# Three small moves in an attention and feed-forward kernel: VectorE's order of sums, a fifth block's PSUM bank, and the split of one product

## The chip, the cores and the metric

One core of a Trainium2 chip. The metric is the device time of one execution in microseconds, lower is better; medians of several runs are quoted. Times are compared within the same rounds.

A ratio of two kernels is the mean time of the one's runs over the mean of the other's in the same rounds, so it is not quite the ratio of the medians.

## The reference, cut to what matters

```python
# q, k, v: (8, 8, 1024, 64); E, F: (64, 1024); w_in: (512, 2048); w_out: (2048, 512)
k_proj = E @ k;  v_proj = F @ v                      # per batch and head, 1024 -> 64
attn   = softmax(q @ k_proj.T / 8)                   # 64 columns
x      = (attn @ v_proj), heads side by side         # (8192, 512)
h      = np.maximum(x @ w_in, 0.0)
out    = (h * h) @ w_out                             # float32
```

## The kernel before: the parts that the change touches

The kernel goes through 8 batches `b`; each has two chunks `ch` of 512 tokens. A chunk has a first stage (16 blocks of `x @ w_in`, each 4 matmuls of 512 columns, then ReLU on ScalarE and the square on VectorE) and a second stage, which makes `(h*h) @ w_out` with seven products in place of eight: the quarters of `h*h` are first added and subtracted on VectorE (the "sums" `s0` to `s3`), as are those of `w_out` (`T1` to `T4`). Attention of the next batch is put between the steps of both stages. The tiles `ps_...` lie in PSUM banks: the kernel's matmuls write them, and ScalarE or VectorE then reads them (VectorE's add of a `ps_y` tile at 79.00 us of the profiled run takes 0.68 us).

```python
def sums(hsq, s, q4, which):          # q4: first or second half of the feature blocks
    ...
    for o, x, y, op in (
        (0, a21, a22, ALU.add), (1, s[0][:, js], a11, ALU.subtract),
        (2, a11, a21, ALU.subtract), (3, a12, s[1][:, js], ALU.subtract),
    ):
        if o in which:
            nc.vector.tensor_tensor(out=s[o][:, js], in0=x, in1=y, op=op)
...
def operands_after(k):                # after the square of pair k
    if b and 4 <= k < 7:
        operands(0, (k - 4,))
    if b and k == 7:
        operands(0, (3,))
        operands(1, (0,))
...
def step1(k, n):
    ...
    if b < 2 or k % 2:
        ps = ffn_psum("ps_h")         # 4 banks in batches 0 and 1, one block each
    ...
    first(ch, HFB * h + j, ps, range(NCB))
    square(k, n, ps)
...
before = range(2) if (b, ch) == (0, 0) or 1 < b < B - 1 else lo     # lo = range(0, 4)
...
def p2a():                            # first part of the second product
    if b:
        operands(1, (1,))
    product(st["x"], st["A12"], W21, before, True)
def p1c():
    product(st["y"], st["A11"], W11, range(7, 8))
    if b == 1:
        operands(1, (3, 2))
    st["a"] = part_pool.tile([P, 2, MH], F32, name="p_a")
    copy(st["a"], "y")                # ScalarE
def p5(js): ... product(st["z"], st["s"][0], T1[:], js, ...)        # then copy to p_d
def p6(js): ... product(st["y"], st["s"][1], T2[:], js)             # goes on in the bank that p_a was read from
def p7(js): ... product(st["y"], st["s"][2], T3[:], js)             # then VectorE: o1 = y + p_d
def p2b():                            # last part of the second product
    product(st["x"], st["A12"], W21, range(before.stop, HFB))
    add(st["o0"][:, :, 0:MH], "x", st["a"])
    if b > 1:
        operands(1, (2, 3))
    ...
def p4(js): ... product(st["y"], st["A22"], T4[:], js)              # goes on in the bank that VectorE just read
...
# batches 0 and 1:
second = [p1a, p2a, p1b, p1c] + lohi(p5) + lohi(p6) + lohi(p3) + lohi(p7) + [p2b] + lohi(p4)
```

The first, fourth, sixth and seventh products all accumulate in one bank `ps_y` without clearing it, so the kernel has each after the first wait until the copy or add that reads the state before it is through (the add at 79.00 us is through at 79.68, and the next `ps_y` matmul starts at 79.73). In batches 0 and 1, `p2b` (bank `ps_x`) covers the read between `p7` and `p4`, with 0.87 us of matmuls there.

Batch 1's attention is placed by step (32 is the first step of the second stage of chunk (0,0)):

```python
BATCH_1 = {
    33: "project 1", 34: "copy_kp, transpose_q, copy_vp", 37: "copy_v_down",
    48: "scores 0, scores 1, exponentials 0", 49: "exponentials 1",
    51: "scores 2, scores 3, exponentials 2", 52: "exponentials 3",
    ...
```

`project` needs K and V of batch 1, which are loaded behind all weights (in the profiled run the last of the weights is issued at 27.59 us, K at 29.09 and V at 30.38). Its K and V matmuls write different halves of one tile's rows; where both operands are there, the two of a pair start within 5 ns of each other (48 pairs after 56 us in the profiled run). `copy_vp` is two copies on ScalarE.

The softmax here doesn't subtract the row's maximum and nothing guards it: scores larger than these inputs give would overflow.

## Time and profile before

| | before |
|---|---|
| time, median of 3 runs | 482.01 us (481.49 to 482.94) |
| span of the profiled run | 480.1 us |
| TensorE / VectorE / ScalarE busy | 98% / 65% / 52% |
| TensorE without idle time | from 53.30 us to the tail |

The page's busy line, the table of stretches, TensorE's timeline at 20 and 52 us, the chain of waits and VectorE's timeline are shown in the prediction. In the timeline a piece begins where its first instruction starts. In the chain of waits a TensorE piece begins where the piece before it *ends*, some 0.16 us later, since the records of matmuls overlap (one of 512 columns is 379 ns long, the next starts after 216). Lengths agree in both.

### The profile page before, as it was taken

Reading aid. Unit: us, or ns where it says so; the run is one execution under the profiler, and the core shown is the slowest. Engines: PE = TensorE matmul, PEld = TensorE weight load, DVE = VectorE, ACT = ScalarE, POOL = GpSimd, SP = SyncE. Lnnn points to the kernel's source line nnn. Section 1 sums busy time; section 2 is a strip of 40 time slices with the busy share of each in tenths; the row PEclk is TensorE's granted clock in tenths of the full one; section 3 lists DMA queues with packets and bytes.
Section 4 is the critical chain, followed back from the end, with each engine's and each line's share of the span. In section 5 each row is a group of like instructions: output and inputs, shape, how many; then the busy total and the mean of one; then the engine's idle time right before and its main releaser. Section 6 shows DMA issues by size and latency. Waiting matters only on the chain.

```text
span 480.1 us, 8400 instructions
## 1 busy us (share of the span) xinstructions
PE 468.3 (98%) x3630; PEld 294.0 (61%) x3630; DVE 314.4 (65%) x382; ACT 247.8 (52%) x365; POOL 34.8 (7%) x48
## 2 busy tenths in 40 slices
PE   4899999999999999999999999999999999999997
PEld 2544686475664756648475574846657475766656
DVE  1478955554957659584695838857485856959383
ACT  2387544758416564375634756156652666334352
POOL 6440020020020100001000100000000000000000
PEclk9999999999999999999999999999999999999999
DMA  9999989579979997209952199223402002020202
GB/s 159 203 204 207 168 183 200 138 117 226 168 113 239 141 209 140 88 1 147 223 81 89 19 178 206 49 87 62 127 1 82 6 1 88 1 89 0 89 1 87
DMA packets 72789, 55.46 MB, mean 116 GB/s; under 512 B 33968, under 2 KB 64944, under 8 KB 72752
## 3 DMA queue, kind: packets, MB, share of 16 engines
q0 software_dynamic: 30624, 29.36, 39.8%
q1 hardware_dynamic: 42128, 25.56, 21.2%
q8 instruction: 28, 0.46, 0.4%
q14 instruction: 9, 0.07, 0.0%
HBM read 59.24 MB, written 16.78 MB: 158 GB/s over the span
## 4 chain that ended last, share of the span: by engine, by line
PE 88%; DMA 9%; POOL 1%; issue 0%; ACT 0%; POOLq 0%
PE ps_h L507 23%; PE ps_y L527 22%; PE ps_att L507 17%; PE ps_z L527 16%; DMA V_sb<-in_v_dram 7%; PE ps_kv L216 2%; PE ps_att L258 2%; PE ps_att L527 2%; DMA w_in<-in_moe_w_in_dram 2%; PE ps_att L243 2%; PE ps_x L527 1%; PE ps_kv L217 0%; POOL V_sb L120 0%; POOL K_sb L120 0%; POOL Q_sb L124 0%
## 5 line engine op out<-in xcount | busy, mean ns | idle before, releaser
L571 DVE TENSOR_TENSOR hsq<-h_relu 128x1024 bf16<-128x1024 f32 x123 | 149.9, 1222 | 79.1 <-ACT h_relu L563 62.5
L507 PEld LDWEIGHTS <-w_in 128*128 128x128 bf16 x1024 | 99.6, 98 | 117.9 <-issue 1.9
L507 PE MATMUL ps_h<-xT,w_in 128*128 128x512 bf16 x640 | 147.8, 379 | 0.2 <-DVE xT L390 0.2
L527 PEld LDWEIGHTS <-s 128*128 128x128 bf16 x1024 | 99.1, 98 | 16.2 <-issue 4.8
L561 ACT ACTIVATE h_relu<-ps_h 128x512 f32<-128x512 f32 x159 | 92.3, 596 | 24.2 <-PE ps_h L507 24.0
L507 PE MATMUL ps_att<-xT,w_in 128*128 128x512 bf16 x384 | 90.7, 379 | 0.0
L527 PEld LDWEIGHTS <-hsq 128*128 128x128 bf16 x768 | 73.8, 98 | 16.5 <-issue 6.0
L563 ACT ACTIVATE h_relu<-ps_att 128x1024 f32<-128x1024 f32 x48 | 49.1, 1023 | 55.4 <-PE ps_att L507 55.4
L527 PE MATMUL ps_y<-T,s 128*128 128x256 bf16 x480 | 57.7, 273 | 0.0
L521 DVE TENSOR_TENSOR s<-hsq 128x1024 bf16<-128x1024 bf16 x64 | 43.5, 683 | 0.0
L285 DVE TENSOR_TENSOR xT<-ps_att,rs 128x1024 bf16<-128x1024 f32 x28 | 33.0, 1214 | 0.6 <-PE ps_att L258 0.6
L657 DVE TENSOR_TENSOR o_sb<-ps_z,p_b 128x512 f32<-128x512 f32 x16 | 11.1, 691 | 33.4 <-PE ps_z L527 27.5
L527 PE MATMUL ps_z<-T,s 128*128 128x256 bf16 x256 | 30.9, 273 | 0.0
L527 PE MATMUL ps_z<-w_out,s 128*128 128x256 bf16 x256 | 30.7, 273 | 0.0
L527 PE MATMUL ps_y<-w_out,hsq 128*128 128x256 bf16 x240 | 30.5, 273 | 0.0
L651 ACT COPY o_sb<-ps_y 128x512 f32<-128x512 f32 x15 | 8.7, 578 | 40.2 <-PE ps_y L527 40.1
L527 PE MATMUL ps_y<-T,hsq 128*128 128x256 bf16 x240 | 29.0, 273 | 0.0
L250 ACT ACTIVATE expT<-ps_att 128x1024 bf16<-128x1024 f32 x28 | 27.7, 1029 | 1.9 <-PE ps_att L243 1.9
L657 DVE TENSOR_TENSOR o_sb<-ps_y,p_d 128x512 f32<-128x512 f32 x15 | 10.4, 690 | 21.4 <-issue 19.7
L651 ACT COPY p_b<-ps_y 128x512 f32<-128x512 f32 x15 | 8.8, 588 | 27.0 <-PE ps_y L527 27.0
L521 DVE TENSOR_TENSOR s<-s,hsq 128x1024 bf16<-128x1024 bf16 x32 | 21.8, 685 | 0.4
L521 DVE TENSOR_TENSOR s<-hsq,s 128x1024 bf16<-128x1024 bf16 x32 | 21.8, 683 | 0.0
(86 smaller groups left out, 277.4 us busy)
## 6 DMA issues: line engine op xcount, KB each, us to landing
out_dram<-o_sb SPq DMA_DIRECT2D x30, 512.0 KB, 3.4
K_sb<-in_k_dram POOLq DMA_DIRECT2D x7, 1024.0 KB, 10.7
V_sb<-in_v_dram POOLq DMA_DIRECT2D x7, 1024.0 KB, 17.8
Q_sb<-in_q_dram POOLq DMA_DIRECT2D x7, 1024.0 KB, 10.4
w_out<-in_moe_w_out_dram POOLq DMA_DIRECT2D x4, 512.0 KB, 13.8
w_in<-in_moe_w_in_dram POOLq DMA_DIRECT2D x7, 256.0 KB, 10.4
K_sb<-in_k_dram POOLq DMA_DIRECT2D x2, 512.0 KB, 8.3
out_dram<-o_sb SPq DMA_DIRECT2D x3, 256.0 KB, 2.1
```

The costliest lines, as they stand in the source:

```text
L216: nc.tensor.matmul(ps[0:KP, :], lhsT=ET[:, i, :], rhs=kv[:, :, i, :], start=f, stop=l)
L243: nc.tensor.matmul(ps[o, bank, :], lhsT=self.kT[r, 2 * pr + j, :], start=True, stop=True, rhs=self.qT[r, NT * (2 * pr + j):NT * (2 * pr + ...
L250: nc.scalar.activation(e[:], self.ps["s", pr][:], AF.Exp, scale=SCALE)
L285: nc.vector.tensor_tensor(out=self.xT[:, 2 * g + e].rearrange("p a n t -> p a (n t)"), in0=self.ps["v", g, e][:], in1=self.rs[g][:], op=AL ...
L507: nc.tensor.matmul(ps[:], lhsT=w_in_blk(cb, fb), rhs=xT[:, cb, :, 2 * ch:2 * ch + 2], start=(cb == 0), stop=(cb == NCB - 1),)
L521: nc.vector.tensor_tensor(out=s[o][:, js], in0=x, in1=y, op=op)
L527: nc.tensor.matmul(ps[tb] if len(ps) == 2 else ps[0][:, tb], lhsT=lhs[:, j, tb * P:(tb + 1) * P], rhs=rhs[:, j], start=first and n == 0 an ...
L561: nc.scalar.activation(r[:, n], ps[:], AF.Relu)
L563: nc.scalar.activation(r[:], st["h"][:], AF.Relu)
L571: multiply = lambda: nc.vector.tensor_tensor(out=o, in0=r[:], in1=r[:], op=ALU.mult)
L651: nc.scalar.copy(to[:, t], ps)
L657: nc.vector.tensor_tensor(out=to[:, t], in0=ps, in1=more[:, t], op=ALU.add)
```

## The change

The intent: take away short holes in TensorE's stream. The fifth block of the very first chunk need not wait for the first block's bank; the last part of the second product covers more of VectorE's add; and VectorE makes the sums that are wanted first, first.

```diff
@@ operands_after
                 if b and k == 7:
-                    operands(0, (3,))
                     operands(1, (0,))
@@ step1
-                if b < 2 or k % 2:
+                if (b, ch, k, n) == (0, 0, 2, 0):
+                    ps = att_psum([P, TCH], F32)
+                elif b < 2 or k % 2:
                     ps = ffn_psum("ps_h")
@@ chunk
-            before = range(2) if (b, ch) == (0, 0) or 1 < b < B - 1 else lo
+            before = lo if b == B - 1 else range(3 if b + ch in (1, 2) and b < 2 else 2)
@@ p1c
                 if b == 1:
+                    operands(0, (3,))
                     operands(1, (3, 2))
@@ p2b
                 if b > 1:
-                    operands(1, (2, 3))
+                    operands(1, (2,))
+                    operands(0, (3,))
+                    operands(1, (3,))
```

## The prediction

> **What bounds the kernel now.** I read the page's busy shares first, then the table of stretches, then TensorE's timeline around the one place where it idles, then the chain of waits from that place on, and last VectorE's timeline beside the chain.
>
> The busy line and the mean rows of the page:
>
> ```profile
> PE 468.3 (98%) x3630; PEld 294.0 (61%) x3630; DVE 314.4 (65%) x382; ACT 247.8 (52%) x365; POOL 34.8 (7%) x48
> ...
> L507 PE MATMUL ps_h<-xT,w_in 128*128 128x512 bf16 x640 | 147.8, 379 | 0.2 <-DVE xT L390 0.2
> ```
>
> TensorE is busy in 98% of the span, and no other engine is above 65%. The 379 ns of one matmul is its latency; the chain below shows the pace, 1.73 us for eight (216 ns) and 1.75 us for sixteen half-width ones (109 ns). So only a hole in the pace of TensorE is worth anything. The table of stretches shows where holes are (PE busy against the length of the stretch; last column GB/s):
>
> ```profile
> 0.00:16.00 16.00, 8.41 (x74) 5.26 (x75) 4.33 (x11) 3.08 (x4) 9.20 (x17) 1.00 1.04 170
> 16.00:53.30 37.30, 36.48 (x321) 17.23 (x321) 28.28 (x37) 28.12 (x47) 9.90 (x13) 1.00 1.26 205
> 53.30:82.30 29.00, 28.99 (x296) 22.57 (x296) 17.50 (x27) 12.24 (x17) 2.62 (x3) 1.00 0.98 178
> 82.30:112.35 30.05, 30.05 (x226) 18.09 (x224) 16.85 (x22) 18.62 (x29) 2.63 (x3) 1.00 0.74 140
> ```
>
> From 53.30 us on TensorE has no idle time at all. Before that it has some, with the transfers at 205 GB/s and the engines for them full. TensorE's timeline of that part:
>
> ```profile
> 20.71 6.40 PE L507 MATMUL ps_h<-xT,w_in 128*128 128x512 bf16 x28 [0.19 <-DVE xT L390]
> ...
> 51.72 1.04 PE L527 MATMUL ps_y<-w_out,hsq 128*128 128x256 bf16 x8
> 52.68 0.40 PE L216 MATMUL ps_kv<-K_sb,ET 128*64 128x512 bf16 x1
> 53.31 0.38 PE L217 MATMUL ps_kv<-V_sb,FT 128*64 128x512 bf16 x1 [0.23 <-DMA V_sb<-in_v_dram]
> ```
>
> Two things are to be seen. The first run of 28 blocks takes 6.40 us where 27 x 0.216 + 0.38 = 6.21 us would do: 0.19 us is lost in it, at the fifth block, which wants the bank of the first. And the first matmul on batch 1's V starts 0.63 us after the K matmul before it, not 0.22: TensorE waits some 0.4 us for V to land. The chain of waits agrees that this is a DMA edge, and shows the three small holes that the change aims at later:
>
> ```profile
> 30.38 22.89 DMA V_sb<-in_v_dram
> ...
> 78.91 0.87 PE ps_x L527 x8
> 79.79 0.98 PE ps_y L527 x8
> ...
> 109.00 0.87 PE ps_x L527 x8
> 109.88 0.94 PE ps_y L527 x8
> ...
> 138.94 0.87 PE ps_x L527 x8
> 139.82 1.82 PE ps_y L527 x16
> ```
>
> Eight half-width matmuls take 0.87 us; the ones after the ps_x piece take 0.98 and 0.94, and sixteen take 1.82 instead of 1.75. These are the fourth sums' product starting on a ps_y bank that VectorE is still reading. VectorE's timeline has that read:
>
> ```profile
> 79.00 0.68 DVE L657 TENSOR_TENSOR o_sb<-ps_y,p_d 128x512 f32<-128x512 f32 x1
> ...
> 109.04 0.69 DVE L657 TENSOR_TENSOR o_sb<-ps_y,p_d 128x512 f32<-128x512 f32 x1 [1.66 <-PE ps_y L527]
> ...
> 138.98 0.69 DVE L657 TENSOR_TENSOR o_sb<-ps_y,p_d 128x512 f32<-128x512 f32 x1
> ```
>
> Each starts as the ps_y product before it ends (within 0.1 us) and lasts 0.69 us; with the way there and back that is just over the 0.87 us of ps_x work that covers it.
>
> [...]
>
> **The change, part by part.** No instruction is added or removed; three things move.
>
> 1. *Fifth block into an attention bank.* Block five of the first chunk no longer waits for the first block's ReLU: 0.19 us less at about 24 us. The attention slot it takes was read by the first two of the four normalizations, which open the chunk, so it is free. The next two users of that pool find their slots free too: the transposes at 26.95 us follow the other normalizations (VectorE through with all four by 22.45), the scores at 29.21 us follow a ReLU that is done by 26.3. From then on each user again follows the one two before it, as now. But TensorE then comes to V's wait 0.19 us earlier and waits 0.6 us in place of 0.4: V was issued at 30.38 by a queue that waits for transfers only. Worth at 53.3 us: 0.
>
> 2. *Longer last part.* In chunks (0,1), (1,0) and (1,1) the second product is split 3 + 5 blocks, not 4 + 4. One block is two half-width matmuls, 2 x 0.109 = 0.22 us. The last part grows from 0.87 to 1.09 us, so the three holes, 0.98 - 0.87 = 0.11, 0.94 - 0.87 = 0.07 and 1.82 - 1.75 = 0.07, are all covered, since each is below 0.22. The total work is the same. Sum: -0.25 us. These lie after V's wait on an engine with no idle time left, so they go through to the end.
>
> The price is that what follows the shorter first part comes 0.22 us sooner. In (1,0) the last block of the first product would start at 100.25 instead of 100.47; its operand, VectorE's square of 98.78 + 1.23 = 100.01, is there with 0.2 us to spare. The first sum's second half is finished at 101.21 in the old order and wanted at 101.56 - 0.22 = 101.34: just enough already. In (1,1) both are ready a microsecond before.
>
> 3. *Order on VectorE.* The fourth sum's first half (0.68 us) leaves its place ahead of the first and second sums' second halves, in 14 chunks, and goes behind. Those two come 0.68 us sooner. TensorE waits for neither today (in the waits, no sum stands among its releasers; in the chain the products on them run at 1.75 us each), so this is worth 0 and gives safety to part 2. The moved sum is wanted much later: in the chunk at 187 us it would end near 191.8, and its product starts at 194.9. The sums are 0.68 us pieces before and after, so VectorE's busy time stays at 314 us.
>
> Sum: 482.01 - 0.25 = 481.76. In executions where V lands up to 0.4 us earlier than in this trace, a part of the 0.19 comes through too; the three times of before differ by 1.45 us, so that may well happen in some. I take 0.06 us for it: 481.7.
>
> **Rivals.** *The fifth block's gain goes through.* For it: V's wait is only 0.4 us, and the lowest run is 0.5 us under the median, as an earlier landing would make it. Against: in this trace V is the edge. It would make 481.5. *A new wait takes the place of the old.* With 0.2 us to spare in (1,0), a late square would hold the first product and give back up to 0.2 us; or the moved fourth sum, now queued behind normalizations in batch 1, delays its product. Against: the margins above, and 2 us for the fourth sum. It would make 481.9 to 482.0. *VectorE's order was the real bound,* and some 14 chunks gain 0.1 us each: 480.4. Against: no chunk after batch 1 has a hole besides the 0.1 us at a switch of tile shape, which stays.
>
> **Range and chances.** The estimate moves by 0.05%, and the kernel's own runs by 0.3%, so the range is that of the noise: 480.9 to 482.5. For 2% some 9.6 us would have to come or go; TensorE has no such idle time to give (11.8 us in all, most of it start and tail), and a change that only moves 0.2 us and 0.7 us pieces has nothing to lose it with, barring a slot order that I misread. So 0.01, 0.98, 0.01.
>
> **What would show it.** Right: the run of first blocks is 0.19 us shorter; TensorE's idle time before V's first matmul grows by as much, and that matmul stays near 53.3 us; the pieces after ps_x take 0.87 and 1.75 us, and ps_x itself 1.09 (ten matmuls); all later chunks take the same time as before to 0.01 us. Wrong: V's first matmul moving earlier with TensorE, a new idle time ahead of the first product's last block in (1,0), or pieces of later chunks other than 1.75 us.

482.01 less 0.25 for the three holes is 481.76, and less the 0.06 taken for executions with an earlier V it is 481.7. That V stays where it is when TensorE comes sooner was the estimate. What the trace of before shows for it: the load of V, issued at 30.38 us, landed 22.89 us later; from 28 to 54 us the DMA engines are busy in every slice to 9 tenths or more; and up to that issue the queue's waits ended on transfers, but for 0.25 and 0.80 us at the start and 0.41 us ahead of V's own issue for which no releaser is shown (in the trace of after the profile names TensorE for 0.43 us there).

Two other places have their numbers in the same trace. The "way there and back" of the add at 79.00 us: it starts 0.08 us after the (modelled) end of the product before it, at 78.92, and the next matmul on the bank starts 0.05 us after its end. The "0.1 us at a switch of tile shape": the first matmul of another shape starts 0.20 us after a half-width one in place of 0.11, and 0.31 us after one of 512 columns in place of 0.22.

## The result, and the profile after

| | before | after |
|---|---|---|
| median | 482.0 us (6 runs, 481.45 to 482.94) | 481.75 us (6 runs, 481.7 to 483.26) |
| ratio of the means | 1 | 0.9999, 95% interval 0.9982 to 1.0017 |
| span of the profiled run | 480.1 us | 480.0 us |

The times alone say "the same": the interval is 0.35% wide, 1.7 us. Whether and where the 0.3 us went must be read from the traces. The page of the kernel after, its first line and its busy line:

```profile
span 480.0 us, 8400 instructions
...
PE 468.9 (98%) x3630; PEld 294.5 (61%) x3630; DVE 316.2 (66%) x382; ACT 247.7 (52%) x365; POOL 34.9 (7%) x48
```

Nothing to be learned there except that no engine has become fuller by more than VectorE's 1.8 us. These come with its new order (316.4 us where that is the only edit, 314.5 and 314.9 for the other two parts alone), where the prediction had the 314 us stay; TensorE does not wait for them. TensorE's timeline of the kernel after, at the places that the prediction showed (start, length, instruction, count, idle time before):

```profile
21.27 3.61 PE L507 MATMUL ps_h<-xT,w_in 128*128 128x512 bf16 x16 [0.19 <-DVE xT L390]
24.72 1.03 PE L507 MATMUL ps_att<-xT,w_in 128*128 128x512 bf16 x4
...
53.04 0.40 PE L216 MATMUL ps_kv<-K_sb,ET 128*64 128x512 bf16 x1
53.04 0.40 PE L217 MATMUL ps_kv<-V_sb,FT 128*64 128x512 bf16 x1
```

The sixteen matmuls of the first four blocks begin at 21.27, and the fifth block (now `ps_att`) at 24.72, 3.45 us later, which is 16 x 0.216: the hole at the fifth block is gone. But two things are not as predicted. The first block starts at 21.27 us and not at 20.71, in a part of the kernel that the change does not touch; and the V matmul starts together with the K matmul at 53.04: there is no wait for V at all. So the prediction's own sign, more idle time ahead of V's first matmul, did not come in this trace. The chain of waits of the kernel after shows another one in its place:

```profile
53.24 1.23 DVE hsq L571
...
56.27 0.60 DVE kp L223
...
56.90 0.64 ACT vp L234 x2
...
57.56 0.59 ACT p_a L652
...
58.20 1.91 PE ps_y L527 x16
...
78.73 1.09 PE ps_x L527 x10
79.83 0.87 PE ps_y L527 x8
...
108.71 1.09 PE ps_x L527 x10
109.81 0.87 PE ps_y L527 x8
...
138.58 1.09 PE ps_x L527 x10
139.68 1.75 PE ps_y L527 x16
```

The last six lines answer to those of before: ten `ps_x` matmuls, and behind them 0.87, 0.87 and 1.75 us where 0.98, 0.94 and 1.82 stood. All three holes are gone. The upper lines are new: the sixth product (the `ps_y` piece at 58.20) waits for ScalarE's copy `p_a`, which stands behind the two copies of batch 1's V, which wait for VectorE's copy of K, which comes after the last square and sums. The piece is 1.91 us long; sixteen such matmuls take 1.75.

### The profile page after: what moved, and what is told of

The parts are those of the page before. It is cut to its first block, busy times and chain, and to the rows that moved or that the text cites. A ratio compares the mean times of both kernels' runs of the same rounds, so it can differ in the third digit from the quotient of the medians. Undisturbed runs are those within 1.5% of the kernel's fastest.

```text
span 480.0 us, 8400 instructions
## 1 busy us (share of the span) xinstructions
PE 468.9 (98%) x3630; PEld 294.5 (61%) x3630; DVE 316.2 (66%) x382; ACT 247.7 (52%) x365; POOL 34.9 (7%) x48
## 4 chain that ended last, share of the span: by engine, by line
PE 94%; ACT 2%; DVE 2%; DMA 1%; issue 0%; SPq 0%
PE ps_h L507 28%; PE ps_y L527 22%; PE ps_att L507 17%; PE ps_z L527 15%; PE ps_att L258 2%; PE ps_kv L216 2%; PE ps_att L527 2%; PE ps_att L243 2%; PE ps_x L527 1%; DMA e_f<-in_F_dram 1%; PE ps_k L301 1%; ACT h_relu L561 1%; DVE hsq L571 1%; PE ps_fill L400 1%; ACT expT L353 0%; DVE xT L390 0%
## 5 line engine op out<-in xcount | busy, mean ns | idle before, releaser
L507 PE MATMUL ps_att<-xT,w_in 128*128 128x512 bf16 x388 | 91.7, 379 | 0.0
L652 ACT COPY p_a<-ps_y 128x512 f32<-128x512 f32 x15 | 8.8, 586 | 24.1 <-PE ps_y L527 24.1
```

The costliest lines, as they stand in the source:

```text
L507: nc.tensor.matmul(ps[:], lhsT=w_in_blk(cb, fb), rhs=xT[:, cb, :, 2 * ch:2 * ch + 2], start=(cb == 0), stop=(cb == NCB - 1),)
L652: nc.scalar.copy(to[:, t], ps)
```

## The experiments

To compare traces whose beginnings differ, I count from the start of the first block's first matmul (S, the `ps_h` line at 20 to 22 us) to the start of the last matmul, both from TensorE's timeline; and from the first V matmul of the projection (V0) to that last one. "Wait for V" is V0 less the start of the first K matmul, which is 0.00 where nothing waits. "At the sixth" is how much longer than 109 ns the step from the fifth to the sixth product of chunk (0,0) takes. When TensorE waits for V to land, I say that V binds. All in us.

| kernel | S | wait for V | at the sixth | S to last | V0 to last | median (before in the same rounds) |
|---|---|---|---|---|---|---|
| before | 20.71 | 0.63 | 0 | 455.72 | 423.12 | 482.0 |
| after | 21.27 | 0 | 0.24 | 454.95 | 423.18 | 481.75 (482.0) |
| fifth_alone | 20.58 | 0.73 | 0 | 455.65 | 423.12 | 481.98 (482.11) |
| tail_alone | 21.78 | 0 | 0.24 | 455.26 | 423.28 | 482.37 (482.11) |
| order_alone | 21.60 | 0 | 0.24 | 455.36 | 423.38 | 481.94 (482.11) |
| tail_2_6 | 21.46 | 0 | 0.24 | 455.39 | 423.61 | 482.11 (482.11) |
| before_lateV | 21.39 | 0.93 | 0 | 456.02 | 423.12 | 482.81 (481.58) |
| after_lateV | 22.15 | 0.02 | 0.24 | 454.95 | 423.16 | 482.53 (481.58) |
| before_laterV | 21.31 | 2.53 | 0 | 457.62 | 423.12 | 485.03 (481.61) |
| after_laterV | 20.97 | 2.68 | 0 | 457.36 | 422.91 | 485.41 (481.61) |
| vp_later | 21.62 | 0.22 | 0 | 455.24 | 422.92 | 481.35 (481.58) |
| eased | 21.18 | 0.01 | 0 | 454.80 | 422.58 | 481.49 (481.58) |
| eased2 | 21.14 | 0 | 0 | 454.67 | 422.46 | 481.26 (481.61) |
| eased3 | 20.99 | 0.33 | 0 | 455.20 | 422.87 | 481.37 (481.61) |

All twelve gave correct results. Every verdict from the times is "same" (within 2%). Only the pair with V half a Q later is clearly off its kernel before, by 0.7% (in part by a lower clock, see there); for the rest the intervals are some 0.3 to 0.5% wide and the effects 0.02 to 0.15%. The traces repeat better: V0 to last is 423.12 in all four kernels with the old split in which V binds, and S to last is 454.95 in both traces of the changed kernel in which it does not. Each kernel has one trace.

**The fifth block alone.** Edit: the two `step1` lines of the change only.

> Only the fifth block in an attention bank. My theory: the 0.19 us hole at the fifth block is gone, the three holes after the ps_x pieces (0.11, 0.07, 0.07) stay. What is left of the 0.19 at 58 us depends on which of two waits binds there in this execution: if V of batch 1 lands later than TensorE comes, TensorE waits for V and nothing is left; if V lands earlier (as in the profile of the change), the wait is at the sixth product, some 0.24 us, for ScalarE's copy of the first product, which follows TensorE's last first-stage block by a fixed chain, and all 0.19 is left. Rival: the hole merely moves to the sixth or seventh block (waits for the ReLUs). Time: same as before, within 0.2 us of it, which the noise covers.

TensorE's timeline:

```profile
20.58 3.61 PE L507 MATMUL ps_h<-xT,w_in 128*128 128x512 bf16 x16 [0.19 <-DVE xT L390]
...
52.38 0.40 PE L216 MATMUL ps_kv<-K_sb,ET 128*64 128x512 bf16 x1
53.11 0.38 PE L217 MATMUL ps_kv<-V_sb,FT 128*64 128x512 bf16 x1 [0.33 <-DMA V_sb<-in_v_dram]
```

From the first block to the first K matmul it takes 52.38 - 20.58 = 31.80 us, against 52.68 - 20.71 = 31.97 before: the hole is gone (31.77 or 31.78 in the four other traces with this part and nothing else new ahead of K). It did not move to the sixth or seventh block. In this execution S was early and V bound: TensorE waited 0.73 us for it in place of 0.63. So 0.10 us of the gain went into the wait, as predicted; the other 0.07 is left in S to last, as V's first matmul came that much sooner after S (32.53 us against 32.60). V0 to last is what it was, 423.12.

**The longer last part alone.** Edit: the `before =` line only.

> Only the 3 + 5 split, VectorE's order as before. My prediction's theory: the three holes go, nothing new, VectorE's old order is just early enough in chunk (1,0) (half of the first sum at 101.21, wanted at 101.34). Rival: counted from the instructions' starts, TensorE wants that half about 0.16 us earlier than I took it, so a new wait of 0.05 to 0.1 us stands in the middle of the fifth product of (1,0). Both: the scores of the fourth pair in chunk (0,1) come 0.22 us sooner and wait some 0.04 us for the exponentials. Net -0.15 to -0.21 us from 60 us to 142 us against before.

The three holes went (all three steps from `ps_x` to `ps_y` within 1 ns of 109). But S to last is 455.26, only 0.10 less than with the old split where V does not bind (455.36, the next experiment). The chain of waits, and VectorE's timeline in the same place:

```profile
101.12 1.85 PE ps_z L527 x16
```

```profile
101.17 0.68 DVE L521 TENSOR_TENSOR s<-hsq 128x1024 bf16<-128x1024 bf16 x1
```

The fifth product of chunk (1,0) takes 1.85 us, not 1.75: a step of 0.20 us at 101.72 in its middle, 0.09 too long, where it wants the second half of the first sum. VectorE ends that at 101.85, behind the fourth sum's first half, and the next matmul starts at 101.92. The rival that was named holds: VectorE's old order is too late once the split is moved, and its move in the change repairs just this.

**VectorE's order alone.** Edit: the three `operands` edits only.

> Only VectorE's order. My theory: worth nothing; every piece of TensorE from 56 us to the end takes what it takes before, to 0.02 us, and the fifth block's hole and the three holes after ps_x stay. Rival: some chunk gains or loses 0.05 us or more, times 14.

The chain of waits:

```profile
79.44 0.87 PE ps_x L527 x8
80.32 0.98 PE ps_y L527 x8
```

As before, hole and all; the other two holes are 0.07 and 0.07 as before, and from the sixth product to batch 2's first block it takes 83.27 us in both kernels. Alone, this part is worth nothing. In this trace V did not bind, so it also shows what the kernel before takes then: S to last 455.36 (455.72 with the binding V).

**A split of 2 + 6.** Edit, on the changed kernel: `before = lo if b == B - 1 else range(2)`.

> The whole change, but with the second product split 2 + 6 in the three chunks. My theory: no further gain, as the holes are already covered at 3 + 5, and the price appears: in (1,0) the last block of the first product comes 0.2 us before its square is there and waits as long, and in (0,1) the scores wait 0.2 us more for exponentials. So 0.3 to 0.4 us is given back between 68 and 101 us against the change. Rival (the margin that I gave in the prediction, 0.2 us left at 3 + 5 in (1,0)): no wait there at 2 + 6.

The chain of waits in chunk (1,0), and the one at chunk (0,1)'s scores:

```profile
99.73 0.66 PE ps_y L527 x6
100.39 0.03 issue
100.42 0.39 PE ps_y L527 x2
```

```profile
69.74 0.33 ACT expT L250
...
70.11 0.41 PE ps_att L243 x4
```

Two `ps_y` matmuls take 0.39 us in place of 0.22. The first product's last block waits 0.20 us for the last square. It was moved by 0.22 us, so at 3 + 5 it had about 0.02 us to spare, not the 0.2 of the prediction. At the scores the fourth pair waits for the second pair's exponentials to free its attention slot: the step from one score matmul to the next is 0.25 us too long, against 0.04 in the changed kernel. S to last is 455.39, 0.44 more than the change. 3 + 5 is the better split, by a hair.

**V later, by a quarter of Q.** Edit, on both kernels, for batch 1:

```diff
-                t = {n: load(n, src, b) for n, src in order}
+                if b == 1:
+                    t = {"K_sb": load("K_sb", k, b)}
+                    ...
+                    nc.gpsimd.dma_start(t["Q_sb"][:, 0:2], rows(q, b)[:, 0:2])
+                    t["V_sb"] = load("V_sb", v, b)
+                    nc.gpsimd.dma_start(t["Q_sb"][:, 2:8], rows(q, b)[:, 2:8])
+                else: ...
```

> The kernel before, with a quarter of batch 1's Q loaded ahead of its V, 256 KB at 205 GB/s, so that V lands some 1.2 us later and certainly after TensorE comes. Expected wait for V about 1.6 us; total about 1.0 to 1.2 us longer than before. With this pair the claim 'a gain ahead of V's wait is worth 0' is tested without the jitter.

> The changed kernel with the same late V. If V's landing sets the time, the fifth block's 0.19 us turns into a longer wait for V (longer by what TensorE comes earlier relative to V), and from V's first matmul to the end this one takes 0.16 to 0.25 us less than the kernel before with late V, from the three holes alone. Rival: V's landing moves with TensorE's progress; then V would land earlier by as much.

Inconclusive as a pair: V bound in the first (0.93 us) and not in the second, where the first block started 0.8 us later. The unchanged part of this pair still helps: the second is one more trace of the changed kernel without a binding V, 454.95 again.

**V later, by half of Q.** The same edit with heads 0:4.

> The kernel before with half of batch 1's Q (512 KB) ahead of its V, as a quarter was not enough to make V bind in both of the pair. V lands at about 55.5 to 56.5 us, TensorE waits for it 2 to 3 us, no wait at the sixth product; span some 2 us longer than before.

> The changed kernel with the same. If a gain ahead of a binding V is worth nothing (the prediction's step 1): from V's first matmul to the last matmul 0.21 us less than the other of the pair (the three holes less the small wait at the scores), and the 0.20 us of the fifth block stands only in a longer wait for V, counted from the first block of the first product of the feed-forward part. If it is worth 0.20 also here, V's landing must come earlier by as much.

TensorE's timelines, the old split first:

```profile
53.28 0.40 PE L216 MATMUL ps_kv<-K_sb,ET 128*64 128x512 bf16 x1
55.81 0.38 PE L217 MATMUL ps_kv<-V_sb,FT 128*64 128x512 bf16 x1 [2.13 <-DMA V_sb<-in_v_dram]
```

```profile
52.74 0.40 PE L216 MATMUL ps_kv<-K_sb,ET 128*64 128x512 bf16 x1
55.42 0.38 PE L217 MATMUL ps_kv<-V_sb,FT 128*64 128x512 bf16 x1 [2.27 <-DMA V_sb<-in_v_dram]
```

Now V binds in both. V0 to last is 423.12 and 422.91: 0.21 less, the three holes (0.26) less the small wait at the scores (0.05: two steps there grew by 22 and 26 ns). TensorE is ready for V 31.97 us after S in the one and 31.77 in the other. Of those 0.20 us, 0.15 are in the longer wait, and 0.05 are left, as V's first matmul came 34.45 us after S in place of 34.50.

The pair is not as clean a test as it was meant to be. V's load was issued 0.5 us earlier in the second (32.15 against 32.68), and that is not chance: the half of Q that now goes ahead of it takes the place of batch 0's Q, and waits until TensorE has transposed that. The issuing queue's timeline of the first of the pair:

```profile
31.94 0.75 POOL L780 DMA_DIRECT2D Q_sb<-in_q_dram  x1 [1.62 <-PE ps_att L335]
```

In all four kernels with the later V this load starts 0.30 us after the end of the last of these transposes. So the edit itself ties V's issue to TensorE; the landing moved by only 0.05 us with it. In the fifth block's run above V's load was not tied so (issued at 30.18 us, before these transposes), and 0.07 us was left.

By the times both are 3.4 to 3.8 us slower than the kernel before, more than the 2 us expected, and not to be told apart. Five of the eight runs had a granted clock of 0.996, and these took 485.36 to 486.69 us; the three at 0.999 took 483.82 to 484.42.

**V's copies behind the first product's.** Edit, on the changed kernel:

```diff
-        33: "project 1", 34: "copy_kp, transpose_q, copy_vp", 37: "copy_v_down",
+        33: "project 1", 34: "copy_kp, transpose_q", 36: "copy_vp", 37: "copy_v_down",
```

> The changed kernel with ScalarE's two copies of batch 1's projected V two steps later, behind the copy of the first product. If the 0.24 us wait at the sixth product of chunk (0,0) is ScalarE's copy standing behind those two, it goes: product five to product six without extra, 0.24 us less where V does not bind. Rival: ScalarE waits for something else and the wait stays, or V binds in this execution and shows a wait in place of it.

ScalarE's timeline:

```profile
57.28 0.59 ACT L652 COPY p_a<-ps_y 128x512 f32<-128x512 f32 x1 [3.39 <-PE ps_y L527]
57.89 0.64 ACT L234 CAST vp<-ps_kv 64x256 bf16<-64x256 f32 x2
```

The copy now comes first and waits for TensorE alone; at the sixth product nothing is lost. V0 to last is 422.92 against 423.18 of the change: 0.26 less. S to last shows nothing of it in this execution, for two reasons: V came 0.22 us late, and already inside the fifth block, at 25.3 us, TensorE's weight loads waited for `w_in`. Their waits between 20 and 54 us (total, times, longest):

```profile
PEld L507 <- DMA w_in<-in_moe_w_in_dram: 1.3, 3, 0.6
```

The same list of the changed kernel has no such line. One step within the block took 0.52 us, 0.30 too long. So the fifth block, free of its bank, can meet the landing of its own weights, another fixed event that I had not looked for.

**All small waits eased.** Edit, on the changed kernel: the projection to step 34, the copies of K to 35, those of V to 36, the third and fourth pairs of scores to 52 and 53.

> The changed kernel with batch 1's projection one step later (after the first part of the second product), the copies of its V behind the copy of the first product, and the third and fourth pairs of scores of batch 1 one step later. All three remaining small waits named so far (V's landing up to 0.45 us later than TensorE, 0.24 us at the sixth product, 0.05 us at the scores) should be gone in one profile: 0.3 us less than the change, 0.5 us less than before, from the traces; the times of 5 rounds may not resolve it. Rival: the later scores or the later copies expose a new wait at the sums or at a weight combination.

The waits for V, at the sixth product and at the third pair are gone, but the rival had a point: the first pair of scores waited 0.13 us (the step to it was 0.22 too long, of which 0.09 is the change of tile shape, as in the traces of before and after: 0.20 us in place of 0.11, 0.31 in place of 0.22). S to last 454.80, so 0.15 less than the change and not 0.3. That it waited for K's transposed copy, now later, is an inference from the next run.

**The same, with the first two pairs of scores a step later too.**

> As the eased kernel, but also the first two pairs of batch 1's scores one step later, so that they do not wait for the transposed K. Expected: no wait for V, at the sixth product, at the scores; from the first block to the last matmul 0.3 us less than the change where V does not bind (454.95 us there), so about 454.65. Rival: exponentials are now too late for the sums and a wait of 0.1 us or more appears there.

The chain of waits at the fifth and sixth products:

```profile
56.25 1.75 PE ps_z L527 x16
57.99 1.75 PE ps_y L527 x16
```

None of the waits that were named is left. One that was not named is, in all 14 traces: inside batch 0's attention, at 36.91 us here and 36.69 in the kernel before, the second group's matmuls on `vp` start 0.39 us after the `ones` matmuls before them, where the first group's start 0.12 us after (36.30 to 36.69 and 31.84 to 31.96 in the kernel before): 0.27 us are lost. That is more than any one of the three holes; what it waits for was not looked for. S to last is 454.67, expected was about 454.65: 0.28 less than the changed kernel and 0.69 less than the kernel before, neither with a binding V (for before, the trace of VectorE's order alone stands in). The median is 481.26 against 481.61 of before in the same rounds, ratio 0.9989 with an interval of 0.9974 to 1.0004. This is the shortest S to last and the lowest median of the kernels tried, and still same by the times.

**Without moving the projection.** Edit: V's copies and the scores' third and fourth pairs only.

> The changed kernel with only the copies of V behind the copy of the first product and the third and fourth pairs of scores one step later. Expected: the same 454.65 us from the first block to the last matmul if V does not bind in this execution; up to 0.4 us more if it does. Rival: a new wait at the sums for late exponentials.

No wait at the sixth product or the scores. V came 0.33 us late, and the fifth block lost 0.17 us to its weights, so 455.20. V0 to last is 422.87 against 422.91 of the change with a binding V: the wait at the scores, 0.04. So the projection's place matters in executions such as this one.

## Why the prediction was right, and where its steps were not

The time was right: 481.7 predicted, 481.75 measured, no change that the times could show. That the two lie 0.05 us apart is luck: the median of the kernel before alone was 481.58 to 482.11 in the four sets of rounds. The mechanism of two of its parts was right, and two sizes and two margins were off.

**Longer last part: right, a little mis-sized.** Predicted -0.25; shown -0.21 with V binding (422.91 against 423.12). The missing 0.05 is a wait at batch 1's scores that I had not listed in the price: work that comes earlier on TensorE meets exponentials that do not.

**"Worth at 53.3 us: 0" for the fifth block: right only where V binds.** There, 0.05 and 0.07 of the 0.20 us were left in the two pairs, as V's first matmul came sooner by that. V's landing counted from S differs by up to 1.4 us between traces (31.15 to 32.56 in the six below), so that a landing that follows TensorE is not excluded by two pairs; that nothing of the gain passes a V that stays where it is follows from V0 to last, 423.12 with and without it. But of the six traces in which nothing around the projection was moved (before, after and the first four experiments), V bound in the two with S below 20.8 us and not in the four above 21.2. Without it the whole change is worth 454.95 - 455.36 = -0.41 us: 0.20 of the fifth block (first block to sixth product: 37.13 us without it and 36.93 with it) and 0.21 of the rest. The prediction allowed 0.06 us on average for such executions; what it lacked is that S itself varies between 20.58 and 22.15 us over the 14 traces, more than the 0.6 us by which V bound in its one trace, and that V's landing varies too, from 52.45 to 53.27 us in those six (22.35 to 22.89 us after its issue). One trace shows which edge binds in that execution, not in all. Of the nine traces with the fifth block in the attention bank, two also lost 0.30 and 0.17 us inside that block to the landing of its weights, which takes the gain back on the spot.

**The size of the wait for V.** I put it at 0.4 us, taking 0.22 us as the normal step from a K matmul to a V matmul. Where V is there, they start together (both at 53.04 us in the kernel after), so it was 0.63. Taking V away gains less than that, 455.72 - 455.36 = 0.36, as the wait for ScalarE's copy is right behind it: in the trace of before that wait was hidden, and the prediction did not see it. It follows TensorE's own last block, not the DMA, so what TensorE gains ahead of it is kept (the 37.13 and 36.93 us above).

**VectorE's order "worth 0": right alone, wrong in company.** Alone it is worth nothing. With the longer last part it is worth 0.11 us (455.26 less the 0.20 of the fifth block would be 455.06, against 454.95), of which 0.09 is the one step in chunk (1,0). The prediction's margin there, "just enough already", came from starting times of the chain of waits, which lie 0.16 us after the instructions' starts. The same slip made the 0.2 us to spare for the last square, which the 2 + 6 split measured at 0.02. Both slips happened to be harmless for the sum, since the change has the order with it.

**What it did not see.** The prediction speaks of one place where TensorE idles. The 0.27 us lost at 36.69 us are another, as large as the three holes together, and the change leaves them.

What stays open: the times could not confirm 0.2 or 0.4 us, as runs of one kernel differ by 1.5 to 3 us; how often V, or the fifth block's weights, bind is known from a handful of traces only; and why the first block's start varies was not tried. The traces show that it isn't the loads alone: in the kernel after, batch 0's K, its V and the first part of its Q all landed 0.4 to 0.6 us sooner than in the kernel before, and S was 0.56 us later. What differs is TensorE's pace before S: the eight matmuls on the second half of batch 0's K took 1.06 and 1.50 us in the two of the six traces in which V bound, and 1.90 to 1.92 in the other four. In the other eight traces the two do not always go together (1.90 with S at 20.97), so the pace looks like one source, not the only one.

## What to carry to other kernels

On a full engine, small holes are worth their size only if no fixed event, such as a landing transfer, lies between them and the end; here the fifth block's 0.20 us left 0.05 and 0.07 us where V's landing bound, and all 0.20 where it did not. Look for such an event first, and ask in more than one trace whether it binds. Take margins from the starts of one view, and remember that shifting work earlier by 0.2 us tests every margin below 0.2 us behind it. Where run-to-run noise exceeds the effect, count between two events inside the trace: here that repeated to 0.01 us where whole runs differed by 1.5 and more.
